# Gated mix of softmax attention and linear attention: PSUM split 2+2 for ScalarE and a pair for VectorE, with units handed out singly

## The chip, the cores and the metric

The kernel runs on one core of one Trainium2 chip. The metric is the device time of one execution in microseconds (us). PE is TensorE's matmul stream, PEld its weight loads, DVE is VectorE, ACT is ScalarE, POOL is GpSimd, SP is SyncE, which here only issues DMAs.

## The reference, cut to what matters

```python
g = _sigmoid((x * gate_w).sum(-1, keepdims=True))
a = _A_ref(x, A_wqkv, A_wo)      # softmax attention, 32 heads of 16
b = _B_ref(x, B_wqkv, B_wo)      # linear attention, 32 heads of 16
return g * a + (1 - g) * b

# _A_ref, x: 1 x 2048 x 512
scores = jnp.einsum("bhqd,bhkd->bhqk", q, k) * (Dh ** -0.5)
p = _softmax(scores, axis=-1)
o = jnp.einsum("bhqk,bhkd->bhqd", p, v)

# _B_ref, phi(t) = where(t > 0, t + 1, exp(t)) + 1e-6
num = jnp.einsum("bhqd,bhde->bhqe", pq, kv); den = jnp.einsum("bhqd,bhd->bhq", pq, z)[..., None] + 1e-6
```

Almost all of the work is in `_A_ref`: 32 heads times 2048 x 2048 scores, each of which goes through an exponential.

## The kernel before, in words

**Units.** Softmax attention is cut into 32 rounds: 4 groups of 8 heads (`t8`) x 4 blocks of 512 queries (`qc`) x 2 halves of the heads (`par`). In a round, four heads lie in the four 32-row tiles `j` of PE's array. A unit is one score matmul: 128 keys (block `kb` of 16) x 512 queries of one head, K = 32 rows (16 of them zero), one PSUM bank. A round has 64 units, the kernel 2048. Up to four units of different row tiles run side by side in the array; such a group of matmuls is called a row wave below. The second matmul (`PV`, probabilities times V and a column of ones) runs as a column wave: four matmuls of 17 columns, one per head, that accumulate in bank 7. After a round, `aout` empties bank 7 (DVE transpose at L882, reciprocal L889, two products on POOL at L891 and L894, and for each second round a transpose into `OAT` at L898).

**Two engines for the exponential.** ACT does it exactly (`cand_exp`, L671): one `ACTIVATE` over a set of 3 banks (0 to 2) or of 2 banks (3 and 4) in turn, into 4 slots of `P3` and 4 of `P2`. DVE does it approximately: `cand_op1` (L616) turns one bank into an int16 whose bits are a bf16, `cand_shift` (L638) makes two shifted copies of four such units at once, and the three terms go into PV with three scaled copies of V. A unit on ACT so costs one quarter of a column wave, a unit on DVE three quarters. DVE's units use banks 5 and 6, one at a time each. A key block (four units, one per head) goes either to ACT or to DVE as a whole, and every column wave takes the four heads of one key block and one term.

**Tasks.** The projections of Q, K and V, the linear attention (`t_phik`, `t_mt`, `t_z`, `t_kv`, `t_phiq`, `t_den`, `t_bout`) and the output product (`t_final`) are generators that ask for a bank (5 or 6, shared with DVE's units), issue matmuls in steps, empty the bank on DVE (or partly on ACT) and free it.

**What sets the order.** A planner in the kernel's build keeps a clock for each engine and a made-up duration for each instruction (the numbers in `C(...)`, `dv(...)`, `pe_step(...)`), and emits at each step the candidate that could start first; equal starts go by priority. A change of PE's array mode (row waves, column waves, full array) counts `SWITCH` = 100 ns in its plan. In gaps that it foresees on PE it puts `fill` matmuls on the tile `warm`, while PE's planned use in the last 3413 ns is not over `FILL`. Each engine then executes its own list in that fixed order, with semaphore waits; nothing is decided at run time. A wait stands on the first instruction of a group, so a row wave that holds units for ACT and for DVE starts when all of its banks are free.

## Time and profile before

| what | us |
|---|---|
| median of 3 runs (all three: 784.26, 772.97, 785.1) | 784.26 |
| the profiled execution's own time | 782.08 |
| its span, first to last instruction | 780.2 |
| ACT busy | 728.1 |
| PE busy (matmuls with their pipeline time) | 693.6 |
| DVE busy | 612.8 |
| POOL busy | 121.9 |
| mean granted TensorE clock | 0.942 |

The profiled execution took 782.08 us, of which 1.9 us lie outside the span. A group's line gives its busy time, the mean of one instruction and the idle time before it. A matmul's duration in the trace holds its way through the array, so waves that follow each other overlap; what a wave costs PE is read from the distance between starts. The column PEclk is the share of full clock that TensorE was granted in a stretch.

### The profile page before, as it was taken

Reading aid. Unit: us, or ns where it says so; the run is one execution under the profiler, and the core shown is the slowest. Engines: PE = TensorE matmul, PEld = TensorE weight load, DVE = VectorE, ACT = ScalarE, POOL = GpSimd, SP = SyncE. Lnnn points to the kernel's source line nnn. Section 1 sums busy time; section 2 is a strip of 40 time slices with the busy share of each in tenths; the row PEclk is TensorE's granted clock in tenths of the full one; section 3 lists DMA queues with packets and bytes.
Section 4 is the critical chain, followed back from the end, with each engine's and each line's share of the span. In section 5 each row is a group of like instructions: output and inputs, shape, how many; then the busy total and the mean of one; then the engine's idle time right before and its main releaser. Section 6 shows DMA issues by size and latency. Waiting matters only on the chain.

```text
span 780.2 us, 15784 instructions
## 1 busy us (share of the span) xinstructions
PE 693.6 (89%) x6179; PEld 210.3 (27%) x6260; DVE 612.8 (79%) x979; ACT 728.1 (93%) x657; POOL 121.9 (16%) x186
## 2 busy tenths in 40 slices
...
GB/s 122 308 10 8 2 8 2 2 8 2 8 2 6 4 1 8 2 1 8 2 8 1 21 16 1 21 16 9 14 14 9 14 21 28 2 21 8 16 14 27
DMA packets 27833, 15.43 MB, mean 20 GB/s; under 512 B 19696, under 2 KB 26736, under 8 KB 27760
## 3 DMA queue, kind: packets, MB, share of 16 engines
...
## 4 chain that ended last, share of the span: by engine, by line
PE 44%; DVE 22%; ACT 20%; issue 13%; POOL 1%; DMA 0%; DVEq 0%; ACTq 0%; POOLq 0%; SPq 0%
PE ps L328 44%; ACT P L671 19%; DVE Z L616 13%; DVE Z L638 5%; DVE T L882 1%; ACT eb L906 1%; DVE KT L796 0%; DVE OAT L898 0%; DVE mb L907 0%; DVE outt L1028 0%; DMA out_dram<-outt 0%; PE ps L772 0%; POOL T L894 0%; DVE wA L993 0%; POOL rg L891 0%
## 5 line engine op out<-in xcount | busy, mean ns | idle before, releaser
L671 ACT ACTIVATE P<-ps 128x1536 bf16<-128x1536 f32 x618 | 713.3, 1278 | 32.1 <-PE ps L328 30.5
L616 DVE TENSOR_SCALAR Z<-ps 128x512 int16<-128x512 f32 x504 | 342.7, 684 | 105.8 <-PE ps L328 92.0
L328 PE MATMUL ps<-Qz,KT 32*128 32x512 bf16 x2048 | 317.8, 401 | 40.4 <-ACT P L671 29.5
L638 DVE TENSOR_SCALAR Z<-Z 128x2048 int16<-128x2048 int16 x252 | 174.1, 708 | 2.0
L328 PE MATMUL ps<-Z,Vc 128*17 128x512 bf16 x1512 | 147.2, 404 | 22.8 <-DVE Z L638 9.2
L328 PE MATMUL ps<-P,Vc 128*17 128x512 bf16 x1544 | 157.9, 403 | 0.2
L328 PEld LDWEIGHTS ps<-Qz,KT 32*128 32x128 bf16 x2048 | 77.0, 91 | 267.5 <-ACT P L671 138.3
L328 PEld LDWEIGHTS ps<-P,Vc 128*17 128x17 bf16 x1544 | 37.8, 89 | 92.4 <-issue 82.4
L328 PEld LDWEIGHTS ps<-Z,Vc 128*17 128x17 bf16 x1512 | 35.5, 89 | 97.4 <-DVE Z L638 36.1
L891 POOL TENSOR_TENSOR rg<-rec,gt 128x16 f32<-128x16 f32 x32 | 9.9, 308 | 319.2 <-DVE rec L889 319.2
L909 POOL TENSOR_SCALAR eb<-eb 128x512 f32<-128x512 f32 x32 | 21.1, 659 | 198.0 <-DVE mb L907 143.1
L910 POOL TENSOR_TENSOR phiK<-eb,mb 128x512 bf16<-128x512 f32 x32 | 42.2, 1319 | 2.3
L328 PE MATMUL ps<-xT,wA 128*128 128x512 bf16 x115 | 33.7, 390 | 4.6 <-issue 1.9
L849 POOL TENSOR_SCALAR Vc<-Vc 128x576 bf16<-128x576 bf16 x32 | 22.8, 713 | 81.9 <-DVE Vc L846 80.6
L328 PE MATMUL ps<-warm 128*32 128x512 bf16 (+9 forms) x185 | 31.2, 382 | 1.4 <-POOL warm L370 1.4
L882 DVE STREAM_TRANSPOSE T<-ps 128x512 f32<-128x512 f32 x32 | 22.7, 708 | 11.4 <-PE ps L328 11.3
L907 DVE TENSOR_SCALAR mb<-ps 128x512 f32<-128x512 f32 x32 | 21.7, 679 | 2.5 <-ACT eb L906 1.4
L328 PE MATMUL ps<-wA,xT 128*128 128x128 bf16 x256 | 21.8, 240 | 0.1
L846 DVE CAST Vc<-ps 128x512 bf16<-128x512 f32 x16 | 11.0, 688 | 12.2 <-PE ps L328 12.2
L894 POOL TENSOR_TENSOR T<-T,rg 128x256 bf16<-128x256 f32 x32 | 20.1, 630 | 2.5
L906 ACT ACTIVATE eb<-ps 128x512 f32<-128x512 f32 x32 | 20.4, 637 | 0.0
L328 PE MATMUL ps<-woA,OAT 128*128 128x512 bf16 x61 | 16.8, 382 | 3.0 <-DVE OAT L898 2.9
...
## 6 DMA issues: line engine op xcount, KB each, us to landing
...
woB<-in_B_wo_dram SPq DMA_DIRECT2D x1, 512.0 KB, 10.6
```

Of the source, the lines that this page charges most:

```text
L328: return lambda: nc.tensor.matmul(o, lhsT=l, rhs=r, start=start, stop=stop, skip_group_check=sg)
L616: return C(DV, 400, 607, lambda: nc.vector.tensor_scalar(Z[:, z, 512 * j:512 * (j + 1)], bank(bk), ZB, 0.0, op0=ALU.add, op1=ALU.max), [r_ ...
L638: return C(DV, 300, 602, lambda: nc.vector.tensor_scalar(Z[:, z, :], Z[:, z0, :], float(m), None, op0=ALU.add), [r_Z[z0]], [r_Z[z]], after ...
L671: return C(AC, 500, 427 * n + 49, lambda: nc.scalar.activation(P[:, slot, 0:512 * n], bank(b0, n), ACT.Exp, scale=ESC), [r_bank[b0 + k] fo ...
L846: yield dv(607, lambda: nc.vector.tensor_copy(Vc[:, 0, vs, :, :, 0:16], src), [r_bank[b]], [r_V[vs]])
L849: yield po(750, lambda k=k: nc.gpsimd.tensor_scalar(Vc[:, k, vs].rearrange("p a b c -> p (a b c)"), Vc[:, 0, vs].rearrange("p a b c -> p ( ...
L882: yield dv(607, lambda: nc.vector.transpose(T1[:, a, :], bank(7)), [r_bank[7]], [r_T1[a]])
L894: yield po(800, lambda: nc.gpsimd.tensor_tensor(t2[:, :, 16 * par:16 * par + 16], t1[:, :, 0:16], rg[:, a, :].unsqueeze(2).to_broadcast([1 ...
L906: yield ac(480, lambda: nc.scalar.activation(eb[:, i, :], bank(b), ACT.Exp), [r_bank[b]], [r_eb[i]])
L907: yield dv(607, lambda: nc.vector.tensor_scalar(mb[:, i, :], bank(b), 0.0, 1e-6, op0=ALU.max, op1=ALU.add), [r_bank[b], r_eb[i]], [r_mb[i]])
L909: yield po(700, lambda: nc.gpsimd.tensor_scalar(eb[:, i, :], eb[:, i, :], 1.0, 0.0, op0=ALU.min, op1=ALU.max), [r_eb[i]], [r_eb[i]])
L910: yield po(1300, lambda: nc.gpsimd.tensor_tensor(dst_ap, eb[:, i, :], mb[:, i, :], ALU.add), [r_eb[i], r_mb[i]], dst_res)
```

## The change

- **Banks.** ACT gets two sets of 2 banks (0 and 1, 2 and 3), DVE gets banks 4 and 5 as one pair that is filled and read together, tasks get bank 6 alone. Bank 7 stays the accumulator. `P3` and `P2` become one tile `P` of 10 slots of 1024 columns.
- **Units singly.** Each row tile `j` has its own queue of key blocks in each round. ACT and DVE take units from the heads of those queues (`act_pick`, `d_choose`), not whole key blocks, and DVE's batch of four (one per `j`) may hold different key blocks. DVE's `op1` reads a pair, 1024 columns, in one instruction.
- **Waves of any four.** A column wave takes for each head whichever item (ACT's or one of DVE's three terms) is there first, so that one wave can mix them. Waves of fewer than four are made where ACT's next slot of `P` is still held, or at the end.
- **Planner.** A candidate that would change PE's mode is no longer ranked later for it; `FILL` goes from 0.5 to 0.65; the steps of `t_z` and `t_den` are cut finer; `t_final` loses its due time (33 to 200).
- **End.** The last round's normalisation runs on DVE and not on POOL; the last four output blocks go out through four buffers laid over `wA`, with a semaphore each, in place of the two halves of `outt`.

Counted through the built programs, before and after:

| | before | after |
|---|---|---|
| ACT: exponentials (units in them) | 309 of 3 banks, 308 of 2, 1 of 1 (1544) | 736 of 2 banks (1472) |
| DVE: `op1` (units) | 504 of 512 columns (504) | 288 of 1024 columns (576) |
| DVE: shifts | 252 | 290 |
| PE: score matmuls, in row waves | 2048 in 922 | 2048 in 861 |
| PE: PV matmuls, in column waves | 3056 in 764 | 3200 in 832 (768 of four, 64 of two) |
| PE: changes between row, column and full mode, without the fills | 1245 | 1521 |
| PE: all matmuls | 6262 | 6541 |
| DVE: `op1` that follows straight on another `op1` | 223 | 53 |

DVE in the tenth round, behind a key block's V. `Z<-ps` is `op1` (L616 before, L603 after), `Z<-Z` a shift (L638, L646), `mb` a step of the linear attention, `Vc` the emptying of a V bank, `T` the emptying of the accumulator. Before:

```order
L616 TENSOR_SCALAR Z<-ps 128x512 x3
L638 TENSOR_SCALAR Z<-Z 128x2048
L616 TENSOR_SCALAR Z<-ps 128x512 x2
L638 TENSOR_SCALAR Z<-Z 128x2048
L616 TENSOR_SCALAR Z<-ps 128x512 x2
L638 TENSOR_SCALAR Z<-Z 128x2048
L616 TENSOR_SCALAR Z<-ps 128x512 x2
L638 TENSOR_SCALAR Z<-Z 128x2048
```

After:

```order
L936 TENSOR_SCALAR mb<-ps 128x512
L603 TENSOR_SCALAR Z<-ps 128x1024 x2
L646 TENSOR_SCALAR Z<-Z 128x2048 x2
L603 TENSOR_SCALAR Z<-ps 128x1024 x2
L646 TENSOR_SCALAR Z<-Z 128x2048 x2
L603 TENSOR_SCALAR Z<-ps 128x1024 x2
L646 TENSOR_SCALAR Z<-Z 128x2048 x2
L864 CAST Vc<-ps 128x32x16
```

Four instructions on one bank each and two shifts have become two instructions on the pair and two shifts; where two `op1` stand together, the second reads the banks that the first has just emptied.

PE at about the same place, behind a step of a V projection (`wA,xT`). `Qz,KT` are score matmuls, `P` (`P_21`, `P_22` before) are PV matmuls on ACT's results, `Z,Vc` PV matmuls on DVE's, `warm` a fill. Before:

```order
L328 MATMUL ps<-wA,xT 128x128 x4
L328 MATMUL ps<-Qz,KT 128x512 x4
L328 MATMUL ps<-P_22,Vc 17x512
L328 MATMUL ps<-P_21,Vc 17x512 x3
L328 MATMUL ps<-Qz,KT 128x512 x3
L328 MATMUL ps<-Z,Vc 17x512 x4
L328 MATMUL ps<-Qz,KT 128x512
L328 MATMUL ps<-warm 128x224
L328 MATMUL ps<-Qz,KT 128x512 x4
```

After:

```order
L327 MATMUL ps<-wA,xT 128x128 x4
L327 MATMUL ps<-Qz,KT 128x512 x2
L327 MATMUL ps<-warm 128x160
L327 MATMUL ps<-P,Vc 17x512 x2
L327 MATMUL ps<-Z,Vc 17x512 x2
L327 MATMUL ps<-Qz,KT 128x512 x4
L327 MATMUL ps<-Z,Vc 17x512 x2
L327 MATMUL ps<-P,Vc 17x512 x2
L327 MATMUL ps<-Qz,KT 128x512 x2
```

Row waves now hold two matmuls (ACT's set) or four (with DVE's pair), and column waves mix `P` and `Z`.

PE at the end of the program; `woB` and `woA` are the output product of a block of 128 rows, eight matmuls each. Before:

```order
L328 MATMUL ps<-P_22,Vc 17x512 x2
L328 MATMUL ps<-woB,xnat 128x512 x4
L328 MATMUL ps<-woA,OAT 128x512 x3
L328 MATMUL ps<-woB,xnat 128x512 x4
L328 MATMUL ps<-woA,OAT 128x512 x3
L328 MATMUL ps<-woB,xnat 128x512 x4
L328 MATMUL ps<-woA,OAT 128x512 x3
L328 MATMUL ps<-woB,xnat 128x512 x4
L328 MATMUL ps<-woA,OAT 128x512 x3
L328 MATMUL ps<-P_21,Vc 17x512 x3
L328 MATMUL ps<-P_22,Vc 17x512
L328 MATMUL ps<-woA,OAT 128x512 x4
```

After:

```order
L327 MATMUL ps<-P,Vc 17x512 x2
L327 MATMUL ps<-Z,Vc 17x512 x2
L327 MATMUL ps<-P,Vc 17x512 x2
L327 MATMUL ps<-woB,xnat 128x512 x4
L327 MATMUL ps<-woA,OAT 128x512 x4
L327 MATMUL ps<-woB,xnat 128x512 x2
L327 MATMUL ps<-woA,OAT 128x512 x4
```

Before, 28 matmuls of four output blocks stand ahead of the last PV wave and 4 behind it; after, the last PV wave comes first and 54 matmuls of seven blocks stand behind it.

The diff, cut to its core:

```diff
-    FILL = 0.5
-
-    NP3, NP2, NZ, NQZ, NVQ = 4, 4, 8, 3, 6
+    FILL = 0.65
+
+    NPS, NZ, NQZ, NVQ = 10, 8, 3, 6
...
-        P3 = SB([128, NP3, 1536], BF16, "P3")
-        P2 = SB([128, NP2, 1024], BF16, "P2")
+        P = SB([128, NPS, 1024], BF16, "P")
...
-        semOUT = [SEM(f"s_out{i}") for i in range(2)]
-        out_fill = [0, 0]
+        semOUT = [SEM(f"s_out{i}") for i in range(6)]
+        out_fill = [0] * 6
...
+        DMIN = 3
+
+        def ready(r, kb):
+            t8, qc, par = rounds[r]
+            return (t8, kb // 4) in K_ready and (t8, qc) in Q_ready
+
+        def head(j):
+            while lead[j] < NR and not uq[lead[j]][j]:
+                lead[j] += 1
+            return lead[j]
+
+        def d_unit(j):
+
+            r = head(j)
+            if r < NR and len(uq[r][j]) < DMIN:
+                r += 1
+            if r >= NR or not uq[r][j] or not ready(r, uq[r][j][0]):
...
+            return r, uq[r][j][0]
...
+        def act_pick(n, out_js):
...
+                if j in out_js:
+                    continue
+                c.append((r, -len(uq[r][j]), j))
+            if len(c) < n:
+                if more or out_js or not c:
+                    return None
+            c.sort()
+            return [(r, uq[r][j][0], j) for r, _, j in sorted(c[:n], key=lambda x: x[2])]
...
+        def d_choose(start):
+
+            if d_busy[0] or max(t_free(4), t_free(5)) > start + 30.0:
+                return []
+            cur = d_batch()
+            if cur is None:
+                return []
+            js = sorted(cur["todo"], key=lambda j: (head(j), -len(uq[min(head(j), NR - 1)][j])))
+            got = [(j, d_unit(j)) for j in js]
+            got = sorted([x for x in got if x[1] is not None][:2])
+            return [(cur, j, u, 4 + k) for k, (j, u) in enumerate(got)]
...
         def cand_s():
-            n = st["set"]
-            if set_busy[n]:
+            sset = st["set"]
+            if set_busy[sset]:
                 return None
-            n = next_units(n)
-            if n == 0:
+            b0 = 2 * sset
+            writes = [r_bank[b0], r_bank[b0 + 1]]
+            start = max(PE.free, _avail(PE, [], writes))
+            extra = d_choose(start)
+            units = act_pick(2, {x[1] for x in extra})
+            if units is None and extra:
+                extra = []
+                units = act_pick(2, set())
+            if units is None:
                 return None
-            if n < st["set"] and not all_units_out_after(n):
-                return None
-            units = [unitq[k] for k in range(n)]
...
+            cur, js = dst["op1"][0]
             z = cur["z"]
+            n = len(js)
...
+            zj = Z[:, z, :].rearrange("p (j c) -> p j c", j=4)
+            o = zj[:, js[0]:js[1] + 1:js[1] - js[0], :] if n == 2 else zj[:, js[0], :]
+            i = bank(4, 2).rearrange("p (j c) -> p j c", j=2) if n == 2 else bank(4)
+            return C(DV, 400, 533 * n + 74, lambda: nc.vector.tensor_scalar(o, i, ZB, 0.0, op0=ALU.add, op1=ALU.max),
+                     [r_bank[4 + k] for k in range(n)], [r_Z[z]], after, f"op1 {[cur['units'][j] + (j,) for j in js]}")
...
-            slot = p_pos[sset] % len(p_pend[sset])
-            if p_pend[sset][slot]:
+            slot = p_pos[0] % NPS
+            if p_pend[slot]:
                 return None
-            b0 = 0 if sset == 3 else 3
-            P = P3 if sset == 3 else P2
+            b0 = 2 * sset
...
                 P[:, slot, 0:512 * n], bank(b0, n), ACT.Exp, scale=ESC),
-                [r_bank[b0 + k] for k in range(n)], [r_P[sset][slot]], after, f"exp{n} {units[0]}")
+                [r_bank[b0 + k] for k in range(n)], [r_P[slot]], after, f"exp{n} {units[0]}")
...
+            wave, short = [], False
+            for j in range(4):
+                if not left[r][j]:
                     continue
-                a = _avail(PE, w["reads"], ())
-                if bt is None or a < bt - 1:
-                    best, bt = w, a
-            if best is None:
+                best, bt = None, None
+                for w in pvi[r][j]:
+                    if (t8, w["kb"] // 4) not in V_ready:
+                        continue
+                    a = _avail(PE, [w["res"]], ())
+                    if bt is None or a < bt - 1:
+                        best, bt = w, a
+                if best is None:
+                    short = True
+                else:
+                    wave.append((bt, j, best))
+            if not wave:
                 return None
-            w = best
-            first = st["first"][r]
-            fns = []
-            vq = (t8, w["kb"] // 4)
-            vs = vslot(*vq)
-            for j in range(4):
-                fns.append(mm(ps[32 * j:32 * j + 17, 3584:4096], Vc[:, w["term"], vs, w["kb"] % 4, 2 * j + par, 0:17], w["aps"][j],
-                              start=first, stop=False, sg=True))
+            prio = 600
+            if short or max(x[0] for x in wave) > PE.free + 1000.0:
+                if exps:
+                    if not p_pend[p_pos[0] % NPS]:
+                        return None
+                elif not st["s_done"]:
+                    return None
+                t0 = max(PE.free, min(x[0] for x in wave))
+                wave = [x for x in wave if x[0] <= t0]
+            fns, reads = [], []
+            for _, j, w in wave:
+                vs = vslot(t8, w["kb"] // 4)
+                fns.append(mm(ps[32 * j:32 * j + 17, 3584:4096], Vc[:, w["term"], vs, w["kb"] % 4, 2 * j + par, 0:17], w["ap"],
+                              start=first[r][j], stop=False, sg=True))
+                for x in (w["res"], r_V[vs]):
+                    if x not in reads:
+                        reads.append(x)
...
+            if r == NR - 1:
+                t2 = T2[:, (r // 2) % 2, :].rearrange("p (q d) -> p q d", d=32)
+                yield dv(70, lambda: nc.vector.tensor_tensor(rg[:, a, :], rec[:, a, :], gt[:, qc, :], ALU.mult), [r_rec[a], r_gt], [r_rg[a]])
+                yield dv(340, lambda: nc.vector.tensor_tensor(t2[:, :, 16 * par:16 * par + 16], t1[:, :, 0:16],
+                                                              rg[:, a, :].unsqueeze(2).to_broadcast([128, 16, 16]), ALU.mult),
+                         [r_T1[a], r_rg[a]], [r_T2[(r // 2) % 2]])
+                yield dv(607, lambda: nc.vector.transpose(OAT[:, t8, 512 * qc:512 * (qc + 1)], T2[:, (r // 2) % 2, :]),
+                         [r_T2[(r // 2) % 2]], [r_OAT[t8][qc]])
+                yield ("FLAG", lambda: flags.add(("oat", t8, qc)))
+                yield ("FLAG", lambda: flags.add(("aout", r)))
+                return
...
-            yield pe_step(16, 140, fns, [*r_phiK[4 * qc:4 * qc + 4], *r_Zb], [r_bank[b]])
+            for k in range(4):
+                yield pe_step(4, 140, fns[4 * k:4 * k + 4], [*r_phiK[4 * qc:4 * qc + 4], *r_Zb], [r_bank[b]])
...
-            yield ("WAIT", lambda: qb < 2 or ("f", qb - 2) in flags)
+            ot, r_ot = outt[:, o, :], r_outt[o]
+            if tail:
+                o = 2 + qbl
+                ot, r_ot = wA[:, qbl, 0:D], R(f"outt{o}")
+                r_ot.r, r_ot.tr = dict(r_wA.r), dict(r_wA.tr)
+            else:
+                yield ("WAIT", lambda: qb < 2 or ("f", qb - 2) in flags)
             if tail and qbl % 2 == 1:
-                yield ac(480, lambda: nc.scalar.copy(outt[:, o, :], bank(b)), [r_bank[b]], [r_outt[o]])
+                yield ac(480, lambda: nc.scalar.copy(ot, bank(b)), [r_bank[b]], [r_ot])
             else:
-                yield dv(607, lambda: nc.vector.tensor_copy(outt[:, o, :], bank(b)), [r_bank[b]], [r_outt[o]])
+                yield dv(607, lambda: nc.vector.tensor_copy(ot, bank(b)), [r_bank[b]], [r_ot])
...
-            add_task(t_final(qb, tail=(qb >= 12)), 25 + 2 * (qb // 4), 33, f"F{qb}")
+            add_task(t_final(qb, tail=(qb >= 12)), 25 + 2 * (qb // 4), 200, f"F{qb}")
...
-                        nt = sum(1 for b in (5, 6) if owner[b] == "T")
-                        free = [b for b in free if b < 5 or nt == 0 or (t["dl"] <= now and all(owner[x] != "D" for x in (5, 6)))]
...
-                    a = max(a, PE.free + SWITCH)
-                start = max(c.E.free, a)
+                    start = max(start, PE.free + SWITCH)
                 if c.E is PE and c.prio < 1000:
                     end = max(t_s, start + c.dur)
                     if t_s < start + c.dur + SWITCH and end + SWITCH > max(t_l, t_s) + 40.0:
                         continue
-                key = (max(start, c.E.free + 45.0), -c.prio)
+                key = (max(start0, c.E.free + 45.0), -c.prio)
```

325 lines of the change are left out of this document (135 added, 190 removed).

## The prediction

> **What bounds the kernel now.** I read the table of busy times first, then ACT's groups by shape, and then the stretches of full and of half clock, which the column PEclk gives.
>
> ```profile
> span 780.2 us, 15784 instructions
> PE 693.6 (89%) x6179; PEld 210.3 (27%) x6260; DVE 612.8 (79%) x979; ACT 728.1 (93%) x657; POOL 121.9 (16%) x186
> L671 ACT ACTIVATE P<-ps 128x1536 bf16<-128x1536 f32 x618 | 713.3, 1278 | 32.1 <-PE ps L328 30.5
> L671 ACT ACTIVATE P<-ps 128x1536 bf16<-128x1536 f32 x309 | 460.6, 1491 | 21.6 <-PE ps L328 20.3
> L671 ACT ACTIVATE P<-ps 128x1024 bf16<-128x1024 f32 x308 | 328.7, 1067 | 10.6 <-PE ps L328 10.2
> ```
>
> ACT is busy for 728.1 of 780.2 us, 713.3 of them in exponentials, and when it waits, it waits for PE (30.5 of 32.1). Its idle 52.1 us lie as follows; the columns of the next rows are the stretch, its length, and busy time (with instructions) of PE, PEld, DVE, ACT and POOL, then the granted clock.
>
> ```profile
> 0.00:40.00 40.00, 35.25 (x258) 14.27 (x262) 19.48 (x29) 30.20 (x28) 9.21 (x27) 0.91 0.72 210
> 40.00:760.00 720.00, 647.05 (x5851) 192.08 (x5924) 589.36 (x945) 691.38 (x623) 111.86 (x158) 0.95 0.04 9
> 760.00:780.20 20.20, 11.31 (x77) 3.97 (x74) 3.99 (x7) 6.54 (x8) 0.84 (x2) 0.87 0.08 26
> ```
>
> That is 9.8 at the start, 13.7 at the end and 28.6 in between. The middle splits by clock. I cut it into the ten stretches at half clock and six of those at full clock, and show of each set a row and the sum:
>
> ```profile
> 228.90:239.20 10.30, 9.80 (x65) 2.77 (x66) 6.64 (x10) 7.25 (x7) 0.00 (x0) 0.50 0.01 2
> sum 78.70, PE 76.05 PEld 20.29 DVE 52.47 ACT 58.61 POOL 4.84; mean PE 7.60 PEld 2.03 DVE 5.25 ACT 5.86 POOL 0.48
> 140.20:228.90 88.70, 77.20 (x740) 23.29 (x742) 79.64 (x128) 88.03 (x82) 20.48 (x26) 1.00 0.02 4
> sum 507.00, PE 454.68 PEld 134.78 DVE 420.66 ACT 502.08 POOL 80.06; mean PE 75.78 PEld 22.46 DVE 70.11 ACT 83.68 POOL 13.34
> ```
>
> At full clock ACT idles 4.9 us in 507 (1%): there ACT sets the pace. At half clock it idles 20.1 us in 78.7 (26%): there PE sets it. So the kernel is bound by ACT, with some 20 us lost to the clock and 8.5 to the rest (28.6 - 20.1). What brings the half clock shows in the 3.4 us ahead of a stretch:
>
> ```profile
> 266.50:269.90 3.40, 3.24 (x28) 0.99 (x25) 2.44 (x4) 3.40 (x4) 0.00 (x0) 1.00 0.00 0
> 269.90:273.30 3.40, 1.67 (x20) 0.42 (x19) 3.40 (x6) 3.40 (x4) 2.49 (x2) 1.00 0.00 0
> 273.30:276.70 3.40, 3.40 (x29) 0.55 (x21) 2.18 (x5) 2.39 (x3) 0.84 (x2) 0.50 0.00 0
> 272.18 0.70 DVE L882 STREAM_TRANSPOSE T<-ps 128x512 f32<-128x512 f32 x1
> 272.93 0.73 PE L328 MATMUL ps<-Z,Vc 128*17 128x512 bf16 x8 [1.04 <-DVE T L882]
> ```
>
> PE ran 20 matmuls there, where the full-clock mean is 28 (740 in 88.7 us), because it waited for DVE, and the next 6.8 us went at half clock. Ahead of 228.9 it is 19 matmuls in the same length. DVE's lateness thus costs ACT by way of the clock.
>
> **The change part by part. ACT's instructions.** The two shapes differ by 1491 - 1067 = 424 ns for a bank. The durations overlap, so the cost in a row comes from the busy time: (713.3 - 309 x 0.424) / 618 = 0.942 us for two banks, that is 0.848 for the banks and 0.094 for the instruction (the one single-bank instruction moves this by less than 1 ns). After: 736 x 0.942 = 693.3 us, against 713.3: 72 units less on ACT save 30.5, 118 more instructions cost 11.1. **ACT: -20.0 us**, on the path wherever ACT sets the pace.
>
> **DVE.** The durations are these; the last column is idle time and its releaser:
>
> ```profile
> L616 DVE TENSOR_SCALAR Z<-ps 128x512 int16<-128x512 f32 x504 | 342.7, 684 | 105.8 <-PE ps L328 92.0
> L638 DVE TENSOR_SCALAR Z<-Z 128x2048 int16<-128x2048 int16 x252 | 174.1, 708 | 2.0
> L977 DVE TENSOR_SCALAR wA<-ps 128x128 f32<-128x128 f32 x4 | 1.2, 292 | 0.9 <-PE ps L328 0.7
> DVE Z L616 <- PE ps L328: 92.0, 132, 2.6
> ```
>
> No row has a read of two banks by DVE. From 128 to 512 columns a `TENSOR_SCALAR` out of PSUM grows by (684 - 292) / 384 = 1.02 ns for a column, so 1024 columns take 684 + 523 = 1207 ns by this estimate; the upper end is two reads, 1368; below, nothing in these rows speaks for less than one read's 684. I take 1207, since it is the same operation on the same source. 288 x 1.207 = 347.6 (+4.9); shifts 290 x 0.691 (174.1 / 252) = 200.4 (+26.3); the last round's products +1. DVE goes from 612.8 to 645. It also loses its second bank: where an `op1` follows straight on another (53 times), DVE waits until PE has refilled the pair. A wait of `op1` for PE is 92.0 / 132 = 0.70 us now, so 53 x 0.70 = 37 us that can't be filled; elsewhere a shift (0.69) or another instruction covers it. 645 + 37 = 682. The cover: DVE idles 86.3 us in the 507 at full clock, 17%, or some 123 us over the 725 from 40 us to the end of the last exponential; of this 69 are used (682 - 613). Off the path, with about 54 us left. At the long read of 1368 it would be 46 less, nearly nothing.
>
> **PE.** The price of a wave and of a mode change, from starts in a stretch at full clock:
>
> ```profile
> 92.46 0.40 PE L328 MATMUL ps<-Qz,KT 32*128 32x512 bf16 x4
> 92.79 0.40 PE L328 MATMUL ps<-Z,Vc 128*17 128x512 bf16 x4
> 93.01 0.39 PE L328 MATMUL ps<-P,Vc 128*17 128x512 bf16 x4
> ```
>
> Row to column takes 0.33 us, column to column 0.22, so a change costs 0.11. Waves go from 922 + 764 = 1686 to 861 + 832 = 1693: +7 x 0.22 = 1.5 us. Changes go from 1245 to 1521: 276 x 0.11 = 30 us. **PE: +32 us.** The cover is PE's idle time at full clock, 52.3 in 507 (10%), some 75 us over 725; it shrinks to 43. The Trainium skill (TensorEngine Tiling, Key Properties) says that changing the tiling mode drains TensorE, which speaks against this change; the rows agree, with 0.11 us. Were it all on the path, the sum below would be 30 us higher, which the second rival holds.
>
> **Waits that are new.** A row wave with DVE's pair stands behind banks 4 and 5 together; on PE the ACT units of that same wave are queued behind it, and ACT behind those. A column wave that mixes terms waits for ACT and for DVE. And ACT's sets give PE 0.94 us to refill each, where the 3-bank set gave 1.37. All three turn DVE's or PE's lateness into ACT's more easily. I scale the 8.5 us of the middle that are not the clock's by PE's cover, 75 / 43: **14.8 us (+6.3)**; ends are 8.5 (the cover suffices) and 29 (as at half clock, 4% of 725).
>
> **The clock.** Matmuls go from 6262 to 6541 in a span that is 2% shorter, so PE has 6.5% more of them in each stretch; 20 in 3.4 us become 21. `FILL` at 0.65 adds fills only in gaps that the planner foresees, and the gaps above are unforeseen. I take 16 us for ACT's idle time at half clock in place of 20.1 (**-4**); ends are 0 and 30.
>
> **The ends.** The rows of the end now:
>
> ```profile
> 761.37 4.20 ACT L671 ACTIVATE P<-ps 128x1536 bf16<-128x1536 f32 x4 [0.19 <-PE ps L328]
> 764.65 0.81 PE L328 MATMUL ps<-woB,xnat 128*128 128x512 bf16 x3 [0.16 <-issue]
> 765.30 0.81 PE L328 MATMUL ps<-woA,OAT 128*128 128x512 bf16 x3
> 770.58 0.40 PE L328 MATMUL ps<-P,Vc 128*17 128x512 bf16 x4
> 773.83 1.04 PE L328 MATMUL ps<-woA,OAT 128*128 128x512 bf16 x4 [2.86 <-DVE OAT L898]
> 777.27 0.58 ACT L1026 CAST outt<-ps 128x512 bf16<-128x512 f32 x1 [2.21 <-DMA out_dram<-outt]
> ```
>
> ACT's last exponential ends at 765.57, and 14.6 us follow. The last PV wave stands behind 28 full matmuls. After the change it comes first (0.5), `aout` runs beside the 54 matmuls that follow (54 x 0.65 / 3 = 11.7, three of them in 0.65), and then the last copy and its DMA come: 0.3 + 0.58 and, from 777.85 to 780.2, 2.35. Sum 15.4: **+0.8**. The waits for the two output buffers (2.2) go with that; the products that move from POOL to DVE, the finer steps of `t_z` and `t_den` and the four outputs on SP are hidden behind those 54 matmuls or stand in the counts above. The start I leave at 9.8: DVE, idle for half of the first 40 us, gets units there, but PE's list has the first PV wave later; bounds -2 and +3, from the 1.7 us by which ACT waited there and the length of a V task's wait (2.94).
>
> ```profile
> 16.37 2.37 ACT L671 ACTIVATE P<-ps 128x1536 bf16<-128x1536 f32 x2 [0.59 <-PE ps L328]
> 19.68 3.83 ACT L671 ACTIVATE P<-ps 128x1536 bf16<-128x1536 f32 x3 [0.95 <-PE ps L328]
> 18.60 0.69 DVE L846 CAST Vc<-ps 128x512 bf16<-128x512 f32 x1 [2.94 <-PE ps L328]
> ```
>
> **Sum.** 780.2 - 20.0 + 6.3 - 4 + 0.8 = 763.3 us of span, with the 1.9 around it **765 us**. Made against 782.08, the profiled execution, which lies 0.3% under the median of 784.26; against that median it is -2.5%.
>
> **Rivals.** *The stalls eat the gain.* ACT saves 20 us of work, but PE's cover falls from 75 to 43 us and DVE's from 123 to 54, the lists are fixed, and each late DVE instruction now holds ACT's units in the same row wave. For: the trace shows this chain (DVE late, PE idle, half clock, ACT idle). Against: from 140.2 to 228.9 DVE was at 90% (79.64 of 88.7) and ACT still at 99%. Price: idle time at full clock 29 in place of 14.8, at half clock 20: 765 + 14 + 4 = 783 us.
>
> *DVE becomes the bound through its single pair (slower).* Place: banks 4 and 5. If the refill of 0.70 us is exposed at each pair and not only at 53, since it has to wait for its turn behind ACT's set and a PV wave on PE, DVE needs 645 + 288 x 0.70 = 847 us. It decides once 645 + n x 0.70 plus the 27 us in which it has no units (11 at the start, 16 at the end) passes ACT's 763, that is n = 130 of 288; at n = 200 the time is 645 + 140 + 27 + 2 = 814 us. For: 163 pairs ride in a wave with ACT's set and so wait for it too. Against: 235 of 288 have another instruction ahead of them that covers most of a refill.
>
> *The clock stays up.* If the denser PE and the fills keep every 3.4 us above what 19 and 20 matmuls mark, ACT's idle time at half clock goes: 765 - 16 = 749 us, 745 if half of the other stalls go too. The Trainium skill (TensorE: Matmul & The Clock Gate, HAM oscillation) says that the clock falls after gaps of more than some 3.4 us between matmul bursts; by that rule there would be no half clock here at all. The trace disagrees: it fell after waits of 1.04 us and less, so the denser stream has to lift whole stretches.
>
> **Chances.** The forecast 0.45 (its own range 752 to 778), the stalls 0.28, DVE the bound 0.15, the clock 0.12. About 2% of 784, that is below 768.6 or above 800, is what runs of this kernel can tell from no change, since its three runs spread over 1.5%. Faster: the clock's 0.12 and three quarters of the forecast's 0.45: 0.46. Slower: most of DVE's case, 0.13. The rest, 0.41, is the same. The range runs from 745 (the clock) to 798 (the stalls with a slow start, DVE's case at n = 176).
>
> **What would show it.** ACT: 736 instructions at 1067 ns and a sum near 693; anything else breaks the first term. DVE: a pair at 1207 ns; its waits for PE at `op1` in number and length say whether the pair is exposed (near 53 waits, or more than 130). PE: waits for ACT small, waits for DVE as now or larger. The stretches at half clock: fewer than 80 us, or more. ACT's idle time from 40 us to 20 us before the end: 31 us by the sum, 49 by the first rival, 15 by the third. The end: some 15 us behind the last exponential. I am wrong if ACT's idle time at full clock exceeds 29 us or if DVE waits at most pairs.

## The result, and the profile after

The changed kernel takes **745.96 us** (median of four runs, 738.14 to 752.72), the kernel before beside it 782.03 us (772.97 to 785.1). The ratio is 0.9506 with a 95% interval of 0.9377 to 0.9635; it leaves out runs that spent unusually long at half clock, which is why it lies a little under the ratio of the medians (0.954). The forecast of 765 us, -2.5%, had the direction; the gain is twice as large, -4.9%. The time lies just inside the range of 745 to 798, at the end that belongs to a rival; the forecast's own range was 752 to 778.

The busy times of the changed kernel's profiled execution (752.72 us, span 750.6, the longest of its four), and its groups by shape:

```profile
span 750.6 us, 16203 instructions
PE 717.4 (96%) x6539; PEld 205.8 (27%) x6539; DVE 657.9 (88%) x803; ACT 703.5 (94%) x775; POOL 124.8 (17%) x184
L668 ACT ACTIVATE P<-ps 128x1024 bf16<-128x1024 f32 x736 | 688.8, 1092 | 27.0 <-PE ps L327 25.0
L603 DVE TENSOR_SCALAR Z<-ps 128x1024 int16<-128x1024 f32 x288 | 350.2, 1216 | 54.8 <-PE ps L327 53.9
L646 DVE TENSOR_SCALAR Z<-Z 128x2048 int16<-128x2048 int16 x290 | 208.7, 741 | 3.6
```

ACT's busy time falls by 24.6 us (728.1 to 703.5), of which 24.5 are exponentials (713.3 to 688.8). ACT's idle time falls by only 5.0 (52.1 to 47.1). Where that lies is in the next two answers: the start, the middle and the end, then the stretches at half clock, one at the start and four behind 40 us (columns as in the prediction's stretches).

```profile
0.00:40.00 40.00, 35.62 (x230) 12.85 (x231) 25.46 (x31) 23.95 (x26) 8.60 (x24) 0.74 0.70 207
40.00:735.52 695.52, 669.51 (x6256) 187.62 (x6254) 626.86 (x763) 678.33 (x748) 116.15 (x160) 0.97 0.04 9
735.52:750.60 15.08, 12.25 (x60) 5.30 (x56) 5.62 (x10) 1.17 (x3) 0.00 (x0) 0.98 0.21 70
```

```profile
10.60:33.10 22.50, 21.25 (x116) 6.44 (x116) 13.05 (x16) 14.05 (x15) 3.29 (x5) 0.54 0.75 238
405.20:425.70 20.50, 20.50 (x158) 5.56 (x150) 14.30 (x22) 15.84 (x17) 0.84 (x2) 0.50 0.00 1
538.30:541.70 3.40, 3.40 (x24) 0.46 (x16) 1.86 (x3) 2.57 (x3) 2.66 (x4) 0.50 0.00 0
579.20:592.90 13.70, 13.70 (x82) 3.44 (x82) 10.18 (x15) 10.93 (x11) 2.27 (x4) 0.50 0.21 44
603.10:609.90 6.80, 6.69 (x61) 1.94 (x60) 5.34 (x7) 5.72 (x7) 0.80 (x2) 0.50 0.10 22
```

| ACT idle, us | before | forecast | after |
|---|---|---|---|
| first 40 us | 9.8 | 9.8 | 16.1 (40 - 23.95) |
| middle, half clock | 20.1 | 16 | 9.3 (44.4 - 35.1, last four stretches) |
| middle, the rest | 8.5 | 14.8 | 7.9 (695.5 - 678.3 - 9.3) |
| end | 13.7 | 14.5 | 13.9 |

The start is longer because this execution was at half clock for 20.5 us of it, from 12.6 to 33.1; the kernel before was for 6.8, and the profiles of the runs below for 0 to 13.7. From the first to the last exponential half clock cost ACT 21.6 us before and 17.8 after. So in these two executions the clock gave 4 us, as forecast; what it gave over all runs is worked out below.

The waits show that PE is now held up more by ACT and less by DVE, first before, then after (engine, line waited for, total, times, longest; PE's waits mostly fall on its weight loads):

```profile
PEld ps L328 <- ACT P L671: 144.2, 330, 1.3
PEld ps L328 <- DVE Z L616: 58.8, 171, 1.0
PEld ps L328 <- DVE Z L638: 38.0, 96, 1.4
```

```profile
PEld ps L327 <- ACT P L668: 213.1, 512, 1.1
DVE Z L603 <- PE ps L327: 53.9, 80, 2.4
PEld ps L327 <- DVE Z L646: 27.7, 79, 1.3
PEld ps L327 <- DVE Z L603: 23.7, 63, 0.8
```

**The clock.** The times of one kernel go with the mean granted clock of the run. The kernel before took 772.6 us at 0.959 and 788.4 at 0.932, 586 us for a unit of clock; the changed one 738.1 at 0.986 and 752.7 at 0.956, 486 for a unit. At nearly one clock the two kernels lie 23 us apart (775.6 at 0.955 against 752.7 at 0.956). The rest of the 36 us between the medians, some 13, goes with the clock, whose median rose from some 0.945 (the kernel before beside the experiments) to 0.975 (five runs of the changed kernel). That is a remainder, and not measured by itself. Times below are medians; "at 0.956" names a single run by its clock.

### The profile page after: what moved, and what is told of

Same layout as the page of the kernel before. It is cut to its first block, busy times and chain, and to the rows that moved or that the text cites. A ratio compares the mean times of both kernels' runs of the same rounds, so it can differ in the third digit from the quotient of the medians.

```text
span 750.6 us, 16203 instructions
## 1 busy us (share of the span) xinstructions
PE 717.4 (96%) x6539; PEld 205.8 (27%) x6539; DVE 657.9 (88%) x803; ACT 703.5 (94%) x775; POOL 124.8 (17%) x184
## 4 chain that ended last, share of the span: by engine, by line
PE 43%; ACT 28%; DVE 16%; issue 13%; ACTq 0%; DVEq 0%
PE ps L327 43%; ACT P L668 28%; DVE Z L603 8%; DVE Z L646 4%; DVE mb L936 1%; DVE T L900 1%; ACT eb L935 0%; DVE Vc L384 0%; DVE OAT L927 0%; DVE Vc L864 0%; DVE QT L836 0%; DVE KT L814 0%; DVE Qz L377 0%; ACTq L1285 0%; DVE Qz L830 0%
## 5 line engine op out<-in xcount | busy, mean ns | idle before, releaser
L668 ACT ACTIVATE P<-ps 128x1024 bf16<-128x1024 f32 x736 | 688.8, 1092 | 27.0 <-PE ps L327 25.0
L603 DVE TENSOR_SCALAR Z<-ps 128x1024 int16<-128x1024 f32 x288 | 350.2, 1216 | 54.8 <-PE ps L327 53.9
L327 PE MATMUL ps<-Z,Vc 128*17 128x512 bf16 x1728 | 233.9, 394 | 6.0 <-DVE T L900 2.5
L327 PE MATMUL ps<-P,Vc 128*17 128x512 bf16 x1472 | 218.2, 396 | 2.8 <-DVE Z L646 1.7
L646 DVE TENSOR_SCALAR Z<-Z 128x2048 int16<-128x2048 int16 x290 | 208.7, 741 | 3.6
L327 PEld LDWEIGHTS ps<-Z,Vc 128*17 128x17 bf16 x1728 | 51.4, 88 | 83.4 <-issue 48.9
L327 PEld LDWEIGHTS ps<-P,Vc 128*17 128x17 bf16 x1472 | 48.1, 88 | 75.5 <-issue 52.7
L327 PE MATMUL ps<-warm 128*32 128x512 bf16 (+14 forms) x347 | 43.3, 319 | 1.4 <-POOL warm L369 1.4
L936 DVE TENSOR_SCALAR mb<-ps 128x512 f32<-128x512 f32 x32 | 21.6, 675 | 0.0
L327 PE MATMUL ps<-xT,wB 128*128 128x512 bf16 x64 | 19.7, 390 | 0.1
L327 PE MATMUL ps<-phiK,xnat 128*128 128x512 bf16 x64 | 19.4, 384 | 0.0
```

The lines of the kernel that those rows point to most:

```text
L327: return lambda: nc.tensor.matmul(o, lhsT=l, rhs=r, start=start, stop=stop, skip_group_check=sg)
L603: return C(DV, 400, 533 * n + 74, lambda: nc.vector.tensor_scalar(o, i, ZB, 0.0, op0=ALU.add, op1=ALU.max), [r_bank[4 + k] for k in range( ...
L646: return C(DV, 300, 602, lambda: nc.vector.tensor_scalar(Z[:, z, :], Z[:, z0, :], float(m), None, op0=ALU.add), [r_Z[z0]], [r_Z[z]], after ...
L668: return C(AC, 500, 427 * n + 49, lambda: nc.scalar.activation(P[:, slot, 0:512 * n], bank(b0, n), ACT.Exp, scale=ESC), [r_bank[b0 + k] fo ...
L936: yield dv(607, lambda: nc.vector.tensor_scalar(mb[:, i, :], bank(b), 0.0, 1e-6, op0=ALU.max, op1=ALU.add), [r_bank[b], r_eb[i]], [r_mb[i]])
```

## The experiments

The expectations name their theories by letters. F is the prediction's: stalls grow as PE's cover, its idle time at full clock, shrinks. Against it stood at first L (DVE's lateness sets the stalls) and W (`FILL` keeps the clock up), and later M (mixed column waves carry the gain), D (the clock follows the density of matmuls), P (the pair carries it) and T (the finer step does). "Stalls" are ACT's idle time at full clock between its first and last exponential: 8.9 us before, 7.9 after. The ratio behind a time is to the kernel before, run beside it, with its 95% interval.

**Fills.** The changed kernel with the old `FILL`:

```diff
-    FILL = 0.65
+    FILL = 0.5
```

> The changed kernel with FILL back at 0.5 (37 fills in place of 113, all else within one or two instructions of it). Theory W (the higher fill level is what keeps TensorE's clock up): half-clock time returns to about the 79 us of the kernel before, ACT idles 10 to 15 us more, 756 to 761 us. Theory L (DVE runs less late against the plan, so PE idles less, and the clock follows): the time stays within 6 us of 746 and the granted clock within 0.015 of the changed kernel's 0.956 to 0.986.

Measured: 746.2 us, ratio 0.9565 (0.9485 to 0.9645), clock 0.968, stalls 9.2. W falls: 76 fills less cost no time, and the profiled execution was at half clock for 37.5 us, not for 79.

**DVE's pair read in two.** The same order of work, two instructions for one:

```diff
-            return C(DV, 400, 533 * n + 74, lambda: nc.vector.tensor_scalar(o, i, ZB, 0.0, op0=ALU.add, op1=ALU.max),
+            fns = [lambda k=k, jj=jj: nc.vector.tensor_scalar(zj[:, jj, :], bank(4 + k), ZB, 0.0, op0=ALU.add, op1=ALU.max)
+                   for k, jj in enumerate(js)]
+            return C(DV, 400, 533 * n + 74, fns,
```

> The changed kernel with the same order of instructions, but DVE's read of the pair made as two reads of one bank each: 288 x (2 x 0.684 - 1.216) = 44 us more on DVE, nothing else. Theory F (the prediction's rule: ACT's stalls grow as PE's cover shrinks): PE's cover is untouched and DVE still has some 35 us left, so 746 to 752 us. Theory L (DVE's lateness against the plan sets the stalls): each pair is 228 ns late in place of 76, PE's waits for DVE double at least, 766 to 790 us with a lower clock.

DVE's and ACT's groups by shape:

```profile
L670 ACT ACTIVATE P<-ps 128x1024 bf16<-128x1024 f32 x736 | 687.6, 1077 | 18.6 <-PE ps L327 17.3
L603 DVE TENSOR_SCALAR Z<-ps 128x512 int16<-128x512 f32 x576 | 368.6, 681 | 39.5 <-PE ps L327 38.9
```

Measured: 751.34 us, ratio 0.9531 (0.9437 to 0.9625), 743.1 at 0.986, stalls 12.2. The single instruction is worth some 5 us (743.1 against 738.1 at 0.986). F's span is met and L's missed; but the edit put only 18 us on DVE (368.6 - 350.2) and not 44, so L was pushed less than intended.

**DVE held at 510 units.** DVE starts no new batch beyond 126 in 32 rounds.

```diff
+                if st["nb"] >= 126 / 32 * (st["issued"] / 64 + 0.5):
+                    return None
```

> The changed kernel with DVE's share held near the 504 units that it had before (255 op1 pairs, 256 shifts, 769 exponentials in place of 288, 290 and 736). ACT gets 33 x 0.936 = 31 us more, DVE 67 us less. If ACT's work sets the time in the changed kernel: 746 + 31 = 777 us. If DVE or PE does: less than 757, for DVE's cover grows.

The same groups:

```profile
L671 ACT ACTIVATE P<-ps 128x1024 bf16<-128x1024 f32 x769 | 719.8, 1121 | 27.7 <-PE ps L327 26.9
L606 DVE TENSOR_SCALAR Z<-ps 128x1024 int16<-128x1024 f32 x255 | 310.7, 1218 | 127.7 <-PE ps L327 127.1
```

Measured: 772.08 us, ratio 0.9917 (0.9872 to 0.9961); stalls 6.1. With 769 exponentials in place of 736 the time is up by 26 us (21 at one clock, 773.9 against 752.7 at 0.956), where 33 x 0.94 = 31 was the price. So ACT's work sets the time. With DVE held near its old share, all the rest of the change together is under 1% faster than the kernel before: DVE's larger share is the gain.

**More for DVE.** The planner is told shorter times for DVE:

```diff
-            return C(DV, 400, 533 * n + 74,
+            return C(DV, 400, 500 * n + 74,
...
-            return C(DV, 300, 602,
+            return C(DV, 300, 560,
```

> The changed kernel planned with DVE's instructions shorter than they are (500 ns a bank and 560 ns for a shift in place of 533 and 602), so that DVE gets 297 pairs and 298 shifts in place of 288 and 290 (+17 us of DVE's time) and ACT 727 exponentials in place of 736 (-8.4 us). If ACT's work alone sets the time: 738. If DVE is at its limit by now (57.6 us idle at full clock, 41 left): stalls of ACT rise by 8 us or more and the time is 746 or more.

Measured: 751.0 us, ratio 0.9685 (0.9628 to 0.9742), stalls 18.2. ACT's busy time fell by 4.0 us to 699.5, and stalls rose by 10.3. So a larger share for DVE no longer pays. Whether DVE has no room left isn't shown: it still idled for 50.4 us at full clock (57.6 in the changed kernel), and a plan with too short times makes it late by itself.

**The rule of order, both ways.** One rule moves between the kernels; in the kernel before it raises mode changes from 1245 to 1463, in the changed one its absence lowers them from 1521 to 1446.

```diff
+                start0 = start = max(c.E.free, a)
                 if c.E is PE and c.mode and c.mode != st["mode"]:
-                    a = max(a, PE.free + SWITCH)
-                start = max(c.E.free, a)
+                    start = max(start, PE.free + SWITCH)
...
-                key = (max(start, c.E.free + 45.0), -c.prio)
+                key = (max(start0, c.E.free + 45.0), -c.prio)
```

> The kernel before with one line of the change: the order in which the planner takes candidates no longer counts the mode change. Mode changes go from 1245 to 1463 and waves from 1686 to 1700: PE +27 us (218 x 0.11 + 14 x 0.22), nearly as much as in the changed kernel. Exponentials 313 + 312 + 1 in place of 309 + 308 + 1, 20 units more on ACT: +9 us. Theory F: PE's cover at full clock falls from 73 to some 46 us, the stalls at full clock rise from 8.9 to 14, time 781 + 9 + 5 = 795. Theory M (cover does not matter, what a wave waits for does): stalls at full clock 7 to 10, time 790 or, where the order frees waves earlier, less. If the rule of order is what brought the gain, the time is under 775.

> The changed kernel with the old rule of order: mode changes 1446 in place of 1521, waves 1709 in place of 1693, so PE -4.7 us; 733 exponentials in place of 736 (-2.8 us), DVE 291 pairs and 292 shifts (+5 us). Theory F: more cover, stalls 7, time 742. Theory M: as the changed kernel less the 3 us of ACT, 743. If the new rule of order carries part of the gain: 755 or more.

Measured: 775.75 us (0.9995, 0.9956 to 1.0034) and 745.61 us (0.9613, 0.957 to 0.9656). The first is 19 us under F's 795, which of the two only M allowed: 218 changes more and 20 units more on ACT did not slow the kernel before, and its stalls were 5.4, not 14. PE's idle time at full clock fell there from 73.3 to 53.1 us, by which F's rule gives 8.9 x 73.3 / 53.1 = 12.3. In the changed kernel 75 changes less gained nothing. F fails here.

**Denser matmuls at one order.** Four matmuls of zeros behind each column wave of the kernel before:

```diff
+            fns += [mm(ps[32 * j:32 * j + 32, 3584:3584 + 128], warm[:, 0:32], warm[:, 0:128], start=False, stop=False, sg=True)
+                    for j in range(4)]
```

> The kernel before in exactly its order, with four more matmuls of zeros over 128 columns behind each of the 764 column waves (they add nothing to the accumulator): 764 x 53 ns = 41 us more work on PE, of which 73 us of idle time at full clock can hide it. It costs time if it does anything to the order. Theory D (the clock follows how densely PE is fed, and the changed kernel is denser): the granted clock rises from 0.945 to between 0.96 and 0.98, and by the 585 us for a unit of clock that the runs of the kernel before show (772.6 at 0.959, 788.4 at 0.932) the time falls by 9 to 20, to 757 to 768, less what the longer waves delay. If the clock follows only how long PE waits, whatever it does otherwise, or something else altogether: clock 0.94 to 0.95, time 776 to 790. Theory F (cover): stalls of ACT at full clock from 8.9 to 20, time 785 to 795.

The busy times, and the row of clock by fortieths:

```profile
PE 717.1 (93%) x9316; PEld 244.4 (32%) x9316; DVE 611.4 (79%) x979; ACT 730.7 (95%) x657; POOL 122.6 (16%) x186
PEclk9999999999999999998999999999899999999998
```

Measured: the clock rose from 0.944 to 0.980 in the median (lowest of ten runs 0.968; of the kernel before the highest of the 17 beside it was 0.959, of all its runs 0.965). Half clock between the first and the last exponential fell from 85 us to 24 in the profiled executions. So D holds for the clock: in one fixed order, matmuls alone raise it. The time, 775.76 us (0.9964, 0.9927 to 1.0), missed D's 757 to 768, since the matmuls also delay. At nearly one clock the kernel took 781.2 at 0.968 against 768.8 at 0.965: 12 us for an estimated 41 us of work, 0.3 each, where the forecast took 6.3 for 32. Stalls went from 8.9 to 14.3. F's rule, with PE's idle time as measured (73.3 to 44.5), gives 14.7: here it fits, and in the run of the rule of order and in the changed kernel it doesn't.

**The split alone.** The kernel before with ACT's sets of two banks, DVE's single reads in banks 4 and 5, whole key blocks and one bank for tasks:

```diff
-            free = [b for b in (5, 6) if owner[b] is None and t_free(b) <= start + 30.0]
+            free = [b for b in (4, 5) if owner[b] is None and t_free(b) <= start + 30.0]
...
-            n = next_units(n)
+            n = next_units(2)
...
-                        free = [b for b in owner if owner[b] is None]
+                        free = [b for b in owner if owner[b] is None and (st["s_done"] or b == 6)]
```

> The kernel before with the bank split alone: ACT two sets of two banks, DVE banks 4 and 5 for itself, still filled and read one at a time, tasks bank 6; key blocks whole, column waves of one block, FILL 0.5. The planner then gives DVE 604 units in place of 504: ACT 722 x 0.94 = 677 us (-36), DVE 604 x 0.684 + 302 x 0.70 + 96 = 720 us (+107), PE 188 waves and 122 mode changes more (+55 us). If the split carries the gain: 745 to 755 us. If the pair read and the single units do (theory L too): DVE is late everywhere, 775 to 800 us.

Measured: 837.67 us, ratio 1.0714 (1.0628 to 1.0801). ACT's busy time fell to 702.8, as low as in the changed kernel, and ACT idled 96.9 us between its first and last exponential. Both spans of the expectation were passed by far. So the split makes the ACT term, and something else has to make it pay.

**Column waves of one kind.** In the changed kernel, all four row tiles from ACT or all from DVE:

```diff
+            for kind in "az":
...
-                    if (t8, w["kb"] // 4) not in V_ready:
+                        if w["name"][0] != kind or (t8, w["kb"] // 4) not in V_ready:
...
+            short, _, wave = min(cands, key=lambda x: (x[0], x[1]))
```

> The changed kernel, but a column wave takes row tiles of one kind only: all from ACT's tiles or all from DVE's. The planner then gives DVE less: 263 pairs and 264 shifts in place of 288 and 290, 761 exponentials in place of 736; column waves 817 in place of 832, row waves 895 in place of 861, mode changes 1480 in place of 1521. ACT's 25 more instructions at 0.94 us are +23.5 us, as the kernel with DVE held at 510 units has shown; PE's work is 0 to +1 us (19 waves more at 0.22, 41 changes less at 0.11). Theory F (stalls grow as PE's cover shrinks): the cover is that of the changed kernel or more, stalls at full clock 6 to 9 us, time 769. Theory M (the mixed waves let PE go on with whatever is ready, and that is why the stalls did not grow): the stalls at full clock rise to 15 to 30 us and PE waits for DVE at its column waves again as in the kernel before; time 777 to 795.

Two of its waits:

```profile
DVE Z L603 <- PE ps L327: 98.7, 102, 7.9
ACT P L668 <- PE ps L327: 67.2, 68, 4.3
```

Measured: 815.41 us, ratio 1.0481 (1.0419 to 1.0542), stalls 39.7; DVE waits for PE up to 7.9 us at a time. M seemed right, though the time lies above its span as well. The mix by itself, in the kernel before; `cand_pv` is that of the changed kernel:

```diff
-                    add_wave(cur["r"], cur["kb"], aps, [r_Z[z]], rel, "t0", 0)
+                    for jj in range(4):
+                        add_item(cur["r"], cur["kb"], jj, Z[:, z, 512 * jj:512 * (jj + 1)].bitcast(BF16), r_Z[z], rel, 0, "z0")
```

> The kernel before with one part of the change alone: a column wave takes any four row tiles that are ready, from ACT's and DVE's tiles and from several key blocks; PSUM's split, the sets of three and two banks, DVE's single reads and its whole key blocks stay. The counts stay too: 616 exponentials for 1540 units in place of 618 for 1544, 508 reads and 254 shifts by DVE in place of 504 and 252, 766 column waves in place of 764, mode changes 1217 in place of 1245. Theory M as it stands (mixed waves take waits from PE wherever they are): PE's and its weight loads' waits for DVE at its reads and shifts fall from 120 us (13.6 + 58.8 + 9.6 + 38.0) to under 90, stalls of ACT at full clock from 8.9 to 5 or 7, the clock rises a little, time 762 to 772. If the mix is only needed because the new split leaves PE without it (short sets, a single pair): time 776 to 782, clock 0.945, stalls 8 to 10 as now.

Measured: 775.37 us, 0.9943 (0.9904 to 0.9982): under 1%, and PE's weight loads waited for DVE as long as before (60.9 and 36.9 us at its reads and shifts, 58.8 and 38.0 before). And both edits together, the mix and the split alone:

> The kernel before with the split alone (ACT's sets of two banks, DVE's single reads in banks 4 and 5, whole key blocks), which took 837.67 us, and now with mixed column waves beside it; counts as there: 722 exponentials, 604 reads and 302 shifts by DVE, 814 column waves, 1070 row waves (1060 there), 1368 mode changes. If mixing is what makes the split pay (theory M with the condition that the split is there): stalls at full clock from 35 to below 15, time 745 to 775. If the split failed for its own work (200 more row waves of PE than in the changed kernel, 44 us, and DVE's single reads): time 820 to 840 as there.

Measured: 837.78 us, 1.0692 (1.0646 to 1.0738), the time of the split alone: the mix gives it nothing.

**Whole key blocks in the changed kernel**, with mixed waves and then with waves of one kind, at equal counts:

```diff
-            return r, uq[r][j][0]
+            cur = dst["cur"]
+            if cur is not None:
+                return cur["claim"] if j in cur["todo"] else None
+            return claim()
```

> The changed kernel, but DVE takes its four units from one key block, as in the kernel before, instead of singly; column waves still mix any four row tiles. 732 exponentials in place of 736 (-3.7 us), 804 column waves in place of 832 and 856 row waves in place of 861 (PE -7.3 us), DVE 292 pairs and 292 shifts (+6.3 us). Theory M (the mixed column waves carry the gain, the single units do not): time 738 to 745, stalls of ACT at full clock 6 to 12 us. If the single units are needed to keep ACT fed: stalls above 20 us, time 755 or more.

> The changed kernel with whole key blocks for DVE, which took 752.35 us, and column waves of one kind. The counts are the same as there: 732 exponentials, 292 pairs, 292 shifts, 804 column waves, 858 row waves (856), 1530 mode changes. So this takes away the mix and nothing else. Theory M: stalls at full clock from 12 to 25 or more, time 775 to 800. If the unmixed kernel above (815) lost its time because single units and waves of one kind don't fit together (fuller buffers, partial waves), and not by the mix itself: time 750 to 757.

Measured: 752.35 us (0.9629, 0.9572 to 0.9686; 743.8 at 0.975) and 742.76 us (0.9502, 0.9464 to 0.954; 742.4 at 0.975). Stalls were 12.4 us in both. M falls: without single units nothing needs the mix, and the kernel with neither is as fast as the changed one (744.1 at 0.975). Single units need mixed waves, mixed waves don't need single units, and the gain needs neither. Of the 69 us that single units lose with waves of one kind, 23.5 are the price of 25 more exponentials; the rest wasn't taken apart.

**The pair.** The split alone with banks 4 and 5 handed over together, and with two of DVE's units allowed in a wave but no pair:

```diff
+                if len(cb) + len(taken) < 2 or len(extra) + len(free) < 2:
+                    break
```

> The kernel before with the split and with DVE's banks 4 and 5 handed over together: PE fills both in one row wave, with ACT's two units or alone, and only when both are free; DVE still reads them one by one; whole key blocks, column waves of one block, the old rule of order and the old end stay. 742 exponentials, 564 reads, 282 shifts, 794 column waves, 912 row waves, 1449 mode changes. Theory P (the split pays because the two banks change hands as a pair, which fills the row waves): stalls at full clock 8 to 15, DVE as busy as in the changed kernel, time 6 us over the changed kernel's for 6 more exponentials, 748 to 765. If some other part of the change is what makes the split pay: 800 to 840, as with the banks handed over singly.

> The same kernel with banks 4 and 5 handed over singly, but a row wave may take two of DVE's units if both banks are free at that time (the run of the split alone took one at most). 718 exponentials, 612 reads, 306 shifts, 818 column waves, 1044 row waves, 1365 mode changes. Theory P: as the split alone, 815 to 840, stalls at full clock above 25. If the split alone failed only because of its limit of one unit a wave: under 770.

Measured: 809.68 us (1.0374, 1.0308 to 1.044) and 823.93 us (1.0576, 1.0508 to 1.0645). P misses its 748 to 765. Of the 92 us between the split alone and the changed kernel (837.7 - 746.0), two of DVE's units in a wave give 14 and the pair another 14. In the split with the pair ACT's timeline then shows one hole:

```profile
654.11 5.72 ACT L672 ACTIVATE P<-ps 128x1024 bf16<-128x1024 f32 x6
698.50 1.94 ACT L672 ACTIVATE P<-ps 128x1024 bf16<-128x1024 f32 x2 [38.66 <-PE ps L328]
```

**The finer step.** In that hole PE ran the denominators (`t_den`) and B's products, the linear attention's, behind them. The edit that looked least: `t_den` in one step of 16 matmuls again, in the changed kernel, and in four of four in the split with the pair.

```diff
-            for k in range(4):
-                yield pe_step(4, 140, fns[4 * k:4 * k + 4], [*r_phiK[4 * qc:4 * qc + 4], *r_Zb], [r_bank[b]])
+            yield pe_step(16, 140, fns, [*r_phiK[4 * qc:4 * qc + 4], *r_Zb], [r_bank[b]])
```

> The changed kernel with one small edit undone: t_den issues its 16 matmuls as one step again, as before, in place of four steps of four. In the trace of the split with the pair ACT stands still for 38.7 us from 659.8, while PE works through the denominators and B's products one after another and the queries of the last rounds wait behind them for the single task bank. Theory T (the planner doesn't put a step of 16 matmuls between two row waves once ACT's sets have two banks, the tasks with one bank pile up behind it, and ACT runs out of queries; the finer step is what lets the split pay): ACT stands still for 30 to 40 us somewhere between 600 and 700 us, time 775 to 795. If the finer step only spread a task that was hidden anyway, as the forecast had it: 740 to 752.

> The kernel before with the split and the pair handed over together (809.68 us), and with t_den in four steps of four. 744 exponentials, 560 reads, 280 shifts, 792 column waves, 922 row waves, 1479 mode changes; single units, mixed waves, the pair read in one instruction, the new rule of order and the new end are all still absent. Theory T: the standstill of 38.7 us goes, time 755 to 772: over the changed kernel's 746 stand 8 more exponentials (7.5), the old end (4) and DVE's two reads (5). If the standstill has another cause: 795 to 812 as there.

The denominators' matmuls (count, shortest, median and longest, first and last start) in the kernel before, the changed kernel, and the changed kernel with the coarse step; with the last queries' copy (`QT`) in the two latter; then, of the last, ACT's first instruction behind its wait, and a stretch:

```profile
L328 PE MATMUL ps<-Zbd,phiK x64: 166/166/180, 428.0 to 599.9; 128*128 128x8 bf16 x64
```

```profile
L327 PE MATMUL ps<-Zbd,phiK x64: 166/166/186, 575.4 to 604.2; 128*128 128x8 bf16 x64
L836 DVE TENSOR_SCALAR QT<-ps x15: 648/679/692, 43.6 to 634.0; 128x512 bf16<-128x512 f32 x15
```

```profile
L327 PE MATMUL ps<-Zbd,phiK x64: 166/167/188, 633.6 to 651.2; 128*128 128x8 bf16 x64
L836 DVE TENSOR_SCALAR QT<-ps x15: 646/683/693, 40.4 to 677.2; 128x512 bf16<-128x512 f32 x15
675.80 1.94 ACT L668 ACTIVATE P<-ps 128x1024 bf16<-128x1024 f32 x2 [40.72 <-PE ps L327]
640.00:650.00 10.00, 6.38 (x39) 2.87 (x40) 4.64 (x7) 0.00 (x0) 0.00 (x0) 0.50 0.41 84
```

Measured: 787.2 us (1.0176, 1.0071 to 1.0281) and 778.8 us (1.0004, 0.9943 to 1.0065; 768.1 at 0.959). Undoing this one edit costs 41 us, 31 at one clock (783.5 against 752.7 at 0.956). Most of the standstill itself ran at half clock (0.50 in the last row), so a comparison at one clock takes part of its cost out.

The planner passes over any step of PE that would push the next row wave past ACT's need. It reckons 997 ns for 16 matmuls and 903 for an exponential of two banks (1330 for three), so the coarse step finds no gap, holds the single task bank, and the last queries wait behind it until ACT has run dry: the denominators start at 633.6, ACT stops at 635.1 (675.80 - 40.72), the last queries come at 677.2 instead of 634.0. T holds for the standstill; that this rule of the planner makes it is read from the code, and no run changed the rule alone.

In the split with the pair the finer step closes the hole as well (ACT's longest wait for PE at an exponential is 1.6 us). But that kernel is only as fast as the kernel before. Its median is 7 us above the expected span, at a clock of 0.936; its runs at 0.96 lie in it, 4 us under the kernel before (772.6 at 0.959) and 15 above the changed one. The expectation reckons 16.5 for eight more exponentials, the old end and two reads, so at one clock the sum comes out. Why the clock of this kernel stays at 0.936, and that of the changed one rises to 0.975, was not found: in each of the runs above and below that undo one part of the change and keep the finer step, the median clock is 0.949 or higher.

**The end.** The changed kernel with the last products on POOL, two output buffers and the old due time:

```diff
-            if r == NR - 1:
+            if False:
...
-            if tail:
+            if False:
```

> The changed kernel with the old end: the last products of the round on POOL, two output buffers, the final tasks with their old due time. The forecast gave the new end +0.8 us and set the wait for the two output buffers at 2.2: time 743 to 750, from the last exponential to the end 13 to 17 us. If the new end brought part of the gain: 752 or more, with the end at 20 us or longer.

Measured: 746.7 us, 0.9569 (0.9508 to 0.9629). From the last exponential to the end it took 20.5 us in place of 15.1, since ACT's copy waited 14.8 us for PE; at one clock the whole kernel is some 4 us slower (747.7 at 0.976 against 744.1 at 0.975). The new end earns a little; of the gain at large it is no part.

## Why the prediction was right or wrong

**Right: the bound and the ACT term's kind.** ACT's work sets the time: 33 exponentials more cost 26 us. The term was -20.0 and measured -24.5: a two-bank exponential takes 688.8 / 736 = 0.936 us in a row, the forecast had 0.942, and over 736 of them that makes 4.5.

**Right: DVE.** The pair read was taken at 1207 ns and measured 1216. DVE's waits for PE at it are 80 in 53.9 us, nearer the 53 (37 us) of the forecast than the 130 from which the single pair would bound the kernel. The shifts became longer (708 to 741 ns), so DVE's busy time rose to 657.9 and not to 645. In the run that gave DVE more, stalls rose.

**Right in kind, with less effect than feared: PE.** PE's busy time rose by 24 us (forecast 32), and its idle time between ACT's first and last exponential at full clock fell from 73.3 to 26.9 (forecast 75 to 43). The Trainium skill (TensorEngine Tiling, Key Properties) has each change of mode drain TensorE; the rows of the prediction agree, with 0.11 us a change, yet 218 changes more in the kernel before moved its time by nothing.

**The step that failed first: "The clock".** The forecast let 20 matmuls in 3.4 us become 21 and took 4 us for it; over all runs the clock gives some 13. It saw that PE gets 6.5% more matmuls in each stretch and gave that little weight, because `FILL` doesn't reach the gaps that bring half clock. The run with added matmuls shows that more matmuls lift the clock, by 0.036, in an unchanged order. It does not show what a higher clock is worth by itself, since those matmuls delay as well.

The forecast also counted the wrong thing. Ahead of the ten stretches at half clock in the middle of the profile before, PE ran 15 to 42 matmuls in 3.4 us, and 24 to 44 ahead of the four after. Ahead of the stretch from 355.2 there were 42, but 24 of them had a single column each (the sums of the linear attention, `t_z`):

```profile
352.08 0.55 PE L328 MATMUL ps<-ones,phiK 128*128 128x1 bf16 x16
353.31 0.35 PE L328 MATMUL ps<-ones,phiK 128*128 128x1 bf16 x8
```

What is low ahead of each fall is how much of the array was filled. Count a matmul's columns, times the share of the array's rows and columns that its form takes (a quarter for a score or a PV matmul). That gives 2040 to 2830 in the 3.4 us ahead of a fall before and 2480 to 2950 after, where stretches of this length that stay at full clock have 4520 and 4810 in the median and some 2700 and 3100 at the least; in the run with added matmuls it is 2130 to 2800 against 5040. This was read from the traces afterwards, and no run tested it. The Trainium skill (TensorE: Matmul & The Clock Gate, HAM oscillation) ties the fall to gaps of more than some 3.4 us; the traces disagree: the longest wait of PE ahead of these falls was 1.12 us.

**The step that failed second: "Waits that are new".** It scaled 8.5 us of stalls by the ratio of PE's cover, 75 / 43, to 14.8; 7.9 were measured, although the cover fell further than forecast. By the same rule the measured cover gives 8.9 x 73.3 / 26.9 = 24. The waits that were to be new did not come: PE's list runs in step with ACT (213.1 us of its weight loads' waits are for ACT, 144.2 before), and DVE's lateness reaches PE half as often (51.4 us of those waits at DVE's two lines, 96.8 before). Which part of the change brings that stays open: with the old rule of order, with the old `FILL`, and with whole key blocks in mixed waves or in waves of one kind, stalls stay at 9.2 to 12.4.

At one clock the forecast had -12.9 (-20.0 + 6.3 + 0.8) and 23 were measured; the clock adds 13 in place of 4. These two differences, 10 and 9, are the 19 us between 765 and 746. The stalls (6.9 less) and the ACT term (4.5 more) account for the 10. What came is nearest to the third rival (749, or 745 with part of the stalls gone), which had a chance of 0.12. Half clock did not vanish, though. Since the clock is either full or half in these traces, a median of 0.945 means some 86 us at half clock and one of 0.975 some 37, by estimate.

**Priced right, and not understood: the finer steps.** The finer steps of `t_z` and `t_den` were set at nothing, "hidden", and cost nothing. But the split can't do without that of `t_den`: without it the change would have been slower than before (787 us, ratio 1.0176, 1.0071 to 1.0281). It is not enough either, as the split with the pair and the finer step shows (778.8 us). The forecast's slower rival looked at banks 4 and 5; the one that the runs showed was the single task bank and a planner that finds no gap for a step longer than ACT's shortened set.
